# Attention with a relative-position bias, then a max-of-three MoE: bias rows of the later heads written during the attention's first steps

## The chip, the core and the metric

The kernel runs on one core of a Trainium2 chip. The metric is device time in microseconds (us) of one execution, as the median of several runs. TensorE is called PE, VectorE DVE, ScalarE ACT, GpSimd POOL and SyncE SP; SP issues nearly all transfers (DMAs), which 16 DMA engines carry out.

## What is computed

```
scores = q @ k^T / sqrt(64)                          # 4 batches, 8 heads, 576 x 576
x      = log1p(|i - j|) / log1p(max(i, 1))           # depends on the positions alone
bias   = max(x * w1 + b1, 0) @ w2                    # 32 hidden values -> 8 heads
attn   = softmax(scores + bias);  out = attn @ v     # -> 2304 tokens of 512
h      = max(out @ mw1, out @ mw2, out @ mw3)        # 768 columns each
result = h @ mwo                                     # 2304 x 512
```

The bias is the same for the four batches, so it is made once, for all eight heads.

## The kernel before

All is written in the order in which each engine runs it; nothing is scheduled behind the author's back.

**Bias stage.** The 576 query positions are 36 groups of 16. For each group, `hidden` makes four tiles on DVE and ACT (L113, L116), `product` multiplies them on PE into a tile of tag `bp` (L134), and `finish` scales that tile into a tile `bs` of 128 partitions (16 positions x 8 heads, L154 on ACT or L157 on DVE, whichever has less work so far) and writes it to `bias_d` in DRAM (L161, 295.5 KB). The groups run as 32 to 35 and then 0 to 31; group g is finished two turns after its hidden tiles. `bs` has 12 buffers. `bp` has four buffers of two PSUM banks, eight banks in all; one more `bp` tile, `wps`, is taken before the first group for five products that only warm PE up. The bias of the first two heads (`load_bias(0, t)`) is read back from `bias_d`, shifted row by row, into the tiles `bias0` to `bias3` (L169, 128 positions each) and `bias4` (L172, the last 64), while the stage runs. `bias1` is loaded after group 21, `bias2` after group 29, `bias3` at the end.

**Attention.** A unit is two heads of one batch, a pair two units. `Attention.step(n)` starts one tile of 128 rows and ends the one of five steps before: `front` multiplies q and k on PE into two score tiles of tag `s` (L262; L255 in every pair's mixed step, which takes the last 64 rows of both units), `shift` adds the bias tile and takes the row extreme on DVE (L272, `sn` and `nm`), `expo` on ACT (L285), `norm` on DVE and POOL (L294, L297). For the older tile, `flip` turns it on PE (L323), and the products with v (L358) follow in the steps after. `s` has two buffers of two banks, which one step fills. Steps 0 to 4 also run four small PE products that fill time (`warm`, L334). The first pair's steps use the bias tiles 0, 1, 2, 4, 2, 3, 3, 0, 1. `load_qk` (L213, L214) and `load_v` (L239, L240) are issued some steps ahead: `load_qk` in steps 0 and 4 for units 2 and 3, `load_v` in step 7 for unit 1.

**Weights.** From step 8 on, the generator `first` converts the expert weights between the steps: `fetch` (L513) loads them one piece ahead, and ACT's `wa` (L520) is the first use. The first `fetch` is issued when the generator is made, ahead of step 0. The tiles of the pools `xa` and `wpool` lie where the bias stage's tiles lay.

**Transfers.** SP issues in program order. Its transfers take eight semaphores in turn (DMAHW0 to 7), so that each waits until the one eight places before it has landed.

**The border.** The stage's SBUF pool `bias_p` and its PSUM pool are released, and the attention's PSUM pool takes the same eight banks; its first two banks are the first buffer of `s`.

Of the kernel before, what the change touches and what calls it, by code (L numbers as in the profile page):

```python
# [9 lines left out]
F32 = mybir.dt.float32  # L10
# [4 lines left out]
PSUM = bass.MemoryType.PSUM  # L15
# [4 lines left out]
def kernel(  # L20
# [12 lines left out]
    nc = tc.nc  # L33
    B, H, S, D = v.shape
# [3 lines left out]
    NTQ = S // 128  # L38
# [3 lines left out]
    NG = S // 16  # L42
# [4 lines left out]
    psums = []  # L47
# [11 lines left out]
    BW = S + 32  # L59
    bias_d = dram.tile([S * H * BW + 2 * S], F32, name="bias_d")  # L60
# [15 lines left out]
    def bias_setup(pool):  # L76
        sm = pool.tile([128, small.shape[1]], F32, name="sm0", bufs=1)
        one = pool.tile([128, 1], F32, name="one", bufs=1)
        w2s = pool.tile([128, 32], F32, name="w2s", bufs=1)
        bp = pool.tile([128, 4 * NG], F32, name="bp", bufs=1)  # L80
        nw = small.shape[1] - S
        nc.scalar.dma_start(out=sm[:, nw:], in_=small[:, nw:])
        nc.sync.dma_start(out=sm[:, 0:nw], in_=small[:, 0:nw])
        nc.scalar.activation(one, signm.bitcast(F32), ACTF.Exp)
        cuts = (0, 1, 3, 35, 35 + 4 * NG, 35 + 5 * NG, 35 + 5 * NG + S)
        w1c, b1c, w2r, pt, ipo, wl = (sm[:, x:y] for x, y in zip(cuts, cuts[1:]))
        nc.vector.tensor_scalar(out=wl, in0=wl, scalar1=w1c, scalar2=None, op0=ALU.mult)
        nc.vector.tensor_scalar(out=w2s, in0=w2r, scalar1=8.0, scalar2=None, op0=ALU.mult)
        nc.scalar.activation(bp, pt, ACTF.Copy, scale=b1c[:, 0:1])
        make_identity(nc, ident)  # L90

        return dict(wl=wl, w2s=w2s, bp=bp, ipo=ipo)

    def bias_stage(pool):
        k = bias_setup(pool)
        wl, w2s = k["wl"], k["w2s"]
        load = {"dve": 0.0, "act": 0.0}
        hid = {}
        late = {}

        def hidden(g):
            i0 = 16 * g
            nf, nr = S - i0, i0 + 15
            n = max(nf, nr + 1)
            n_act = 1 if load["act"] + (n + 90) < load["dve"] + 4 * (0.52 * n + 130) else 0
            load["act"] += n_act * (n + 90)
            load["dve"] += (4 - n_act) * (0.52 * n + 130)
            hs = []
            for c in range(3, -1, -1):
                m = 4 * g + c  # L110
                h = pool.tile([128, S], F32, tag=f"hid{c}", bufs=4, name=f"hid{m}")
                if c < 4 - n_act:
                    nc.vector.tensor_scalar(out=h[:, 0:n], in0=wl[:, 0:n], scalar1=k["bp"][:, m:m + 1],  # L113
                                            scalar2=0.0, op0=ALU.add, op1=ALU.max)
                else:
                    nc.scalar.activation(h[:, 0:n], wl[:, 0:n], ACTF.Relu, bias=k["bp"][:, m:m + 1])  # L116
                hs.insert(0, h)
            hid[g] = (hs, nf, nr)

        def product(g):  # L120
            hs, nf, nr = hid.pop(g)
            bp = psums[-1].tile([128, 1024], F32, tag="bp", bufs=4, name=f"bp{g}")
            o = 512 - nr if max(nf, nr) <= 512 else 0
            if nr > 512:
                runs = [(0, nr, 512, -1), (512, nr - 512, nr - 512, -1), (nr, 0, nf, 1)]
            elif nf > 512:
                runs = [(0, nr, nr, -1), (nr, 0, 512 - nr, 1), (512, 512 - nr, nr + nf - 512, 1)]
            else:
                runs = [(o, nr, nr, -1), (512, 0, nf, 1)]
            late[g] = bp[:, o:o + nr + nf]  # L130
            for o, d, w, step in runs:
                for c in range(4):
                    src = hs[c][:, d:d + w] if step > 0 else hs[c][:, d:d - w:-1]
                    nc.tensor.matmul(bp[32 * c:32 * c + 32, o:o + w], lhsT=w2s, rhs=src, start=True, stop=True)  # L134


        todo = list(range(NG - LEFT // 16, NG)) + list(range(NG - LEFT // 16))
        for i in range(NG + 2):
            if i < NG:
                hidden(todo[i])  # L140
            if 0 < i <= NG:
                product(todo[i - 1])
            if i > 1:
                x = todo[i - 2]
                finish(pool, k, load, x, late.pop(x))
            yield

    def finish(pool, k, load, g, i):
        bs = pool.tile([128, S + 16], F32, tag="bs", bufs=12, name=f"bs{g}")
        ip = k["ipo"][:, g:g + 1]  # L150
        w = S + 15
        o = bs[:, 0:w]
        if load["act"] + 0.96 * w + 165 <= load["dve"] + 1.04 * w + 185:
            nc.scalar.activation(o, i, ACTF.Copy, scale=ip)  # L154
            load["act"] += 0.96 * w + 165
        else:
            nc.vector.tensor_scalar(out=o, in0=i, scalar1=ip, scalar2=None, op0=ALU.mult)  # L157
            load["dve"] += 1.04 * w + 185
        dst = bass.AP(tensor=bias_d.tensor, offset=bias_d.offset + 16 * g * H * BW,
                      ap=[[H * BW + 1, 16], [BW, H], [1, S + 15]])  # L160
        nc.sync.dma_start(out=dst, in_=bs[:, 0:S + 15])  # L161

    def bias_rows(i, n, h, j, w, nh=1):
        ap = [[H * BW, n]] + ([[BW, nh]] if nh > 1 else []) + [[1, w]]
        return bass.AP(tensor=bias_d.tensor, offset=bias_d.offset + (i * H + h) * BW + 15 + j, ap=ap)

    def load_bias(hp, t):
        if t < NTQ:
            nc.sync.dma_start(out=bias_t[t], in_=bias_rows(128 * t, 128, 2 * hp, 0, S, 2))  # L169
        else:  # L170
            for p in (0, LEFT):
                nc.sync.dma_start(out=bias_t[t][p:p + LEFT], in_=bias_rows(LB, LEFT, 2 * hp, 0, S, 2))  # L172
# [16 lines left out]
    LAG = 5  # L189
# [790 lines left out]
    with tc.manual_schedule():  # L980
# [2 lines left out]
        apool = tc.alloc_tile_pool(name="attn_p", bufs=1, side="right")  # L983
        at = Attention(apool)
        n = 0
        with tc.tile_pool(name="bias_p", bufs=1) as bp:
            warm = bp.tile([128, 256], F32, name="warm")
            nc.vector.memset(warm, 0.0)
            wps = psums[-1].tile([128, 1024], F32, tag="bp", bufs=4, name="wps")
            for _ in range(5):  # L990
                nc.tensor.matmul(wps[:, 0:256], lhsT=warm[:, 0:128], rhs=warm, start=True, stop=True)
            for g, _ in enumerate(bias_stage(bp)):
                if g == 0:
                    at.load_qk(0)
                    at.load_v(0)
                    first = at.prep(0)
                if g in (5, 8):
                    next(first)
                if g == 16:
                    at.load_qk(1)  # L1000
                if g == 33:
                    second = at.prep(1, nc.gpsimd)
                if g in (33, 35):
                    next(second)

                if g == 12:
                    load_bias(0, NTQ)
                if g in (19, 27, 35):
                    load_bias(0, (g - 19) // 8)
            load_bias(0, NTQ - 1)  # L1010
        psums.pop().release()
        psums.append(tc.alloc_tile_pool(name="psum", bufs=1, space=PSUM))
        xa = ctx.enter_context(tc.tile_pool(name="xa", bufs=1, reuse_waits="tile"))
        wpool = ctx.enter_context(tc.tile_pool(name="wpool", bufs=1, reuse_waits="tile"))
        for x in range(NX):
# [171 lines left out]
```

## Time and profile before

| | us |
|---|---|
| median of 3 runs | 580.58 (580.0 to 583.82) |
| profiled execution | 579.1 |
| its span, from the first to the last instruction | 577.3 |
| PE busy / DVE / ACT / POOL | 565.7 / 447.4 / 370.9 / 289.6 |
| granted clock of PE, mean | 1.000 of full speed (2.4 GHz) |

Times in the rows are counted from the span's start. A row of a timeline has the start, the time from the first start to the last end, engine, line and tile, and in brackets how long the engine stood still before and what the profile names as its releaser. That releaser is inferred: where an instruction waits for several semaphores, the one that came last by the profile is named. DMA share is the mean busy share of the 16 DMA engines; the landing of a DMA is counted from the start of its issue.

### The profile page before, as it was taken

How to read it: one execution, taken by the hardware profiler on the slowest of the kernel's cores; microseconds unless marked ns; L12 is line 12 of the kernel's file. 1: busy time of each engine (PE TensorE's matmuls, PEld its weight loads, DVE VectorE, ACT ScalarE, POOL GpSimd, SP SyncE). 2: the span in 40 equal slices, each digit the busy share in tenths (PEclk: the TensorE clock that was granted, in tenths of full speed). 3: DMA queues.
4: the chain of work that ended last, by engine and by line, in shares of the span. 5: the costliest groups of instructions: out<-in, count | busy, mean ns of one | idle time of the engine just before them, and what ended most of it. 6: DMA issues, size and time to landing. Idle time of an engine off the chain costs nothing.

```text
span 577.3 us, 12583 instructions
## 1 busy us (share of the span) xinstructions
PE 565.7 (98%) x4593; PEld 463.1 (80%) x4593; DVE 447.4 (77%) x955; ACT 370.9 (64%) x856; POOL 289.6 (50%) x296
## 2 busy tenths in 40 slices
PE   8998999999999999999999999999999999989997
PEld 4455766667676767676759999999999999979997
DVE  7995679999989999888749876664777235798884
ACT  7996898888889988798747553243233233545552
POOL 1856577687787979786640043362472330720000
PEclk9999999999999999999999999999999999999999
DMA  5898804934593456630010131521223132456662
GB/s 162 229 364 300 259 16 96 353 119 161 151 328 98 156 161 200 192 99 22 23 38 1 55 128 37 177 99 37 73 92 123 51 99 66 144 177 181 185 188 77
DMA packets 72493, 79.61 MB, mean 138 GB/s; under 512 B 22896, under 2 KB 53872, under 8 KB 72432
## 3 DMA queue, kind: packets, MB, share of 16 engines
q1 hardware_dynamic: 72288, 78.52, 43.2%
q8 instruction: 36, 0.59, 0.5%
q10 hardware_dynamic: 144, 0.29, 0.2%
q14 instruction: 25, 0.20, 0.1%
HBM read 50.61 MB, written 27.93 MB: 136 GB/s over the span
## 4 chain that ended last, share of the span: by engine, by line
PE 88%; ACT 5%; DVE 2%; issue 2%; POOL 1%; DMA 1%; DVEq 0%; POOLq 0%
PE pv L358 15%; PE tp L323 12%; PE s L262 11%; PE p L581 10%; PE p L580 10%; PE p L579 10%; PE bp L134 3%; PE p_o L906 3%; PE p_o L904 3%; PE p_o L905 3%; PE s L255 2%; PE c L579 1%; PE c L580 1%; PE c L581 1%; ACT hid L116 1%
## 5 line engine op out<-in xcount | busy, mean ns | idle before, releaser
L297 POOL TENSOR_SCALAR e<-e,rc 128x576 f32<-128x576 f32 x144 | 113.5, 801 | 53.9 <-DVE rc L294 41.0
L285 ACT ACTIVATE e<-sn,nm 128x576 f32<-128x576 f32 x144 | 111.4, 775 | 33.2 <-DVE nm L272 29.6
L272 DVE CUSTOM_DVE_ANT_0 sn<-s,bias 128x576 f32<-128x576 f32 x144 | 103.1, 753 | 21.8 <-PE s L262 16.1
L323 PEld LDWEIGHTS tp<-ident,e 128*128 128x128 f32 x576 | 61.6, 141 | 31.4 <-issue 17.8
L323 PE MATMUL tp<-ident,e 128*128 128x128 f32 x576 | 78.9, 280 | 0.4 <-DVE et L406 0.2
L358 PE MATMUL pv<-et,vt 128*64 128x320 f32 (+1 forms) x496 | 75.2, 419 | 0.1
L471 POOL TENSOR_TENSOR wl<-wr,wh 128x256 fp32r<-128x256 f32 x25 | 22.9, 943 | 95.3 <-ACT wh L663 95.3
L406 DVE COPY et<-tp 128x512 f32<-128x512 f32 (+1 forms) x80 | 49.5, 627 | 17.2 <-PE tp L323 16.5
L358 PEld LDWEIGHTS pv<-et,vt 128*64 128x64 f32 x496 | 31.2, 136 | 24.8 <-issue 11.3
L619 ACT COPY u<-p 128x384 f32<-128x384 f32 x24 | 11.5, 479 | 58.9 <-PE p L581 58.8
L262 PE MATMUL s<-kh,qh 64*128 64x288 f32 x256 | 47.6, 343 | 1.2 <-ACT bs L154 0.9
L229 POOL TENSOR_TENSOR kl<-kr,kh 128x576 fp32r<-128x576 f32 x16 | 40.8, 2550 | 15.6 <-ACT kh L226 15.3
L403 ACT COPY et<-tp 128x512 f32<-128x512 f32 (+1 forms) x72 | 39.5, 548 | 7.7 <-PE tp L323 4.8
L134 PE MATMUL bp<-hid,w2s 128*32 128x79 f32 (+51 forms) x640 | 41.1, 394 | 2.0 <-DVE hid L113 1.1
L113 DVE TENSOR_SCALAR hid<-sm,bp 128x528 f32<-128x528 f32 (+17 forms) x108 | 40.2, 449 | 0.0
L262 PE MATMUL s<-kl,qh 64*128 64x288 f32 x256 | 40.2, 295 | 0.0
L262 PE MATMUL s<-kh,ql 64*128 64x288 f32 x256 | 39.4, 290 | 0.2 <-POOL ql L229 0.2
L134 PEld LDWEIGHTS bp<-hid,w2s 128*32 128x32 f32 x640 | 21.0, 110 | 22.6 <-issue 12.9
L262 PEld LDWEIGHTS s<-kh,qh 64*128 64x128 f32 x256 | 26.2, 184 | 12.9 <-issue 5.0
L471 POOL TENSOR_TENSOR wl<-ws,wh 128x256 fp32r<-128x256 f32 x28 | 27.4, 1008 | 14.6 <-ACT wh L665 11.9
L471 DVE TENSOR_TENSOR q<-p,u 128x384 f32<-128x384 f32 x36 | 19.9, 554 | 17.4 <-ACT u L626 14.9
L626 ACT COPY u<-p 128x384 f32<-128x384 f32 x24 | 11.5, 479 | 32.8 <-PE p L581 32.8
(230 smaller groups left out, 1632.8 us busy)
## 6 DMA issues: line engine op xcount, KB each, us to landing
bias_d<-bs SPq DMA_DIRECT2D x36, 295.5 KB, 5.9
bias<-bias_d SPq DMA_DIRECT2D x16, 576.0 KB, 6.2
w<-in_moe_w_dram SPq DMA_DIRECT2D x36, 256.0 KB, 3.1
h_d<-ht SPq DMA_DIRECT2D x18, 384.0 KB, 3.2
hin<-h_d SPq DMA_DIRECT2D x16, 384.0 KB, 4.4
qr<-in_qd_dram SPq DMA_DIRECT2D x16, 288.0 KB, 5.3
kr<-in_kd_dram SPq DMA_DIRECT2D x16, 288.0 KB, 5.3
vt<-in_v_dram SPq DMA_DIRECT2D x32, 128.0 KB, 3.2
```

What stands on the lines that cost most here:

```text
L134: nc.tensor.matmul(bp[32 * c:32 * c + 32, o:o + w], lhsT=w2s, rhs=src, start=True, stop=True)
L262: nc.tensor.matmul(ss[h][:, x, 0:HALF], lhsT=u[q][p, 128 * t:128 * t + 128], rhs=u[k][p, cols], start=(j == 0), stop=(j == 2))
L272: nc.vector.tensor_tensor_reduce(out=sn.rearrange("p (a b) -> p a b", a=2), in0=st["s"][h][:, :, 0:HALF], in1=bt.rearrange("p (a b) -> p a ...
L285: nc.scalar.activation(st["e"][:, S * h:S * h + S], sn, ACTF.Exp, scale=-1.0, bias=nm, accum_out=st["sm"][:, h:h + 1])
L297: nc.gpsimd.tensor_scalar(out=e, in0=e, scalar1=rc[:, h:h + 1], scalar2=1.0, op0=ALU.mult, op1=ALU.mult)
L323: nc.tensor.transpose(tp[:, 128 * c:128 * c + 128], e2[:, k0:k0 + 128], ident)
L358: nc.tensor.matmul(pv[p], lhsT=w, rhs=x, start=(c == 0), stop=(c == NTQ))
L406: nc.vector.tensor_copy(*x)
L471: eng.tensor_tensor(out=out, in0=f(a), in1=f(b), op=op)
L579: nc.tensor.matmul(o, lhsT=hi[:, c], rhs=h[:, j], start=first and j == 0, stop=False, **on)
L580: nc.tensor.matmul(o, lhsT=hi[:, c], rhs=l[:, j], start=False, stop=False, **on)
L581: nc.tensor.matmul(o, lhsT=lo[:, c], rhs=h[:, j], start=False, stop=last and j == 1, **on)
```

## The change

For the last 14 groups of the stage (18 to 31), `finish` writes only the rows of heads 0 and 1, each with a DMA of its own (16 partitions of the tile, every eighth one). The tile is kept (`bs` has 26 buffers), and its whole group, the first two heads included, is written later: three groups at the end of each of steps 2 to 5 and two in step 6. For that, steps 0 to 6 run ahead of the release of `bias_p`, and the pools `xa` and `wpool` and the first `fetch` come after step 6 rather than before step 0. The attention's PSUM pool is made with `reuse_waits="tile"`: a tile in it waits only for what used its own banks, where before the pool's first tile waited for all.

```diff
-                finish(pool, k, load, x, late.pop(x))
+                finish(pool, k, load, x, late.pop(x), i - 2 >= NG - KEPT)
             yield
 
-    def finish(pool, k, load, g, i):
-        bs = pool.tile([128, S + 16], F32, tag="bs", bufs=12, name=f"bs{g}")
+    KEPT = 14
+    kept = []
+
+    def finish(pool, k, load, g, i, keep):
+        bs = pool.tile([128, S + 16], F32, tag="bs", bufs=12 + KEPT, name=f"bs{g}")
...
-        dst = bass.AP(tensor=bias_d.tensor, offset=bias_d.offset + 16 * g * H * BW,
-                      ap=[[H * BW + 1, 16], [BW, H], [1, S + 15]])
-        nc.sync.dma_start(out=dst, in_=bs[:, 0:S + 15])
+
+        def write(h=None):
+
+            dst = bass.AP(tensor=bias_d.tensor, offset=bias_d.offset + 16 * g * H * BW + (h or 0) * BW,
+                          ap=[[H * BW + 1, 16]] + ([[BW, H]] if h is None else []) + [[1, S + 15]])
+            nc.sync.dma_start(out=dst, in_=bs[:, 0:S + 15] if h is None else bs[h::H, 0:S + 15])
+
+        if keep:
+            for h in range(2):
+                write(h)
+            kept.append(write)
+        else:
+            write()
...
-        with tc.tile_pool(name="bias_p", bufs=1) as bp:
+        bp = tc.alloc_tile_pool(name="bias_p", bufs=1)
...
         psums.pop().release()
-        psums.append(tc.alloc_tile_pool(name="psum", bufs=1, space=PSUM))
+        psums.append(tc.alloc_tile_pool(name="psum", bufs=1, space=PSUM, reuse_waits="tile"))
+        while n < LAG + 2:
+            at.step(n)
+            for f in kept[:3] if n > 1 else ():
+                kept.pop(0)()
+            n += 1
+        bp.release()
         xa = ctx.enter_context(tc.tile_pool(name="xa", bufs=1, reuse_waits="tile"))
```

SP's queue at the end of the bias stage, before (`bs29` is group 29's tile, `bias2` the bias tile 2; in brackets the semaphores waited for):

```order
L161 DMA bias_d_60<-bs28_851 16x8x591 [waits DMAHW6_49,Activation_49]
L161 DMA bias_d_60<-bs29_871 16x8x591 [waits DMAHW7_49,Activation_49]
L169 DMA bias2_76<-bias_d_60 128x2x576 [waits DMAHW1_49,DMAHW0_49]
L161 DMA bias_d_60<-bs30_888 16x8x591 [waits DVE_49]
L161 DMA bias_d_60<-bs31_891 16x8x591 [waits DMAHW2_49,Activation_49]
L169 DMA bias3_77<-bias_d_60 128x2x576 [waits DMAHW5_49,DMAHW4_49,DMAHW6_49,DMAHW3_49,DMAHW7_49,DMAHW2_49,DMAHW1_49]
L513 DMA w643_0_918<-in_moe_w1_dram 128x2x256 x2
L213 DMA qr2_922<-in_qd_dram 128x576
```

The same place of SP's queue in the changed kernel:

```order
L167 DMA bias_d_60<-bs29_882 16x591 [waits DMAHW2_49,Activation_49]
L167 DMA bias_d_60<-bs29_882 16x591 [waits DMAHW3_49]
L182 DMA bias2_76<-bias_d_60 128x2x576 [waits DMAHW4_49]
L167 DMA bias_d_60<-bs30_900 16x591 [waits DMAHW5_49,DVE_49]
L167 DMA bias_d_60<-bs30_900 16x591 [waits DMAHW6_49]
L167 DMA bias_d_60<-bs31_904 16x591 [waits DMAHW7_49,Activation_49]
L167 DMA bias_d_60<-bs31_904 16x591 [waits DMAHW0_49]
L182 DMA bias3_77<-bias_d_60 128x2x576 [waits DMAHW5_49,DMAHW3_49,DMAHW6_49,DMAHW2_49,DMAHW7_49,DMAHW1_49,DMAHW0_49]
L226 DMA qr2_914<-in_qd_dram 128x576
```

Each group's write has become two of 16 rows, and the first weights have left the place behind the load of `bias3`. Further down in the same queue of the changed kernel stand the whole groups:

```order
L227 DMA kr2_913<-in_kd_dram 128x576
L167 DMA bias_d_60<-bs18_646 16x8x591 [waits DMAHW4_49]
L167 DMA bias_d_60<-bs19_667 16x8x591
L167 DMA bias_d_60<-bs20_688 16x8x591
L167 DMA bias_d_60<-bs21_709 16x8x591
L167 DMA bias_d_60<-bs22_731 16x8x591
L167 DMA bias_d_60<-bs23_752 16x8x591 [waits DMAHW1_49]
L226 DMA qr3_1052<-in_qd_dram 128x576 [waits DMAHW2_49,PE_49,Pool_49]
```

They stand between the loads of `qr`/`kr` for unit 2 and for unit 3, and eight more follow behind the latter; DMAHW4 is here the load of `bias2` and DMAHW1 that of `bias3`. On PE, the first score of the attention follows the last products of group 31. Before:

```order
L134 MATMUL bp31_879<-hid127_854,w2s_96 32x80
L262 MATMUL s0_0_0_925<-kh0_242,qh0_318 128x288 [waits DVE_49,Activation_49]
L262 MATMUL s0_0_1_926<-kh0_242,qh0_318 128x288
L262 MATMUL s0_0_0_925<-kl0_243,qh0_318 128x288 [waits Pool_49]
L262 MATMUL s0_0_1_926<-kl0_243,qh0_318 128x288
```

In the changed kernel:

```order
L134 MATMUL bp31_891<-hid127_865,w2s_96 32x80
L275 MATMUL s0_0_0_917<-kh0_242,qh0_318 128x288 [waits Activation_49]
L275 MATMUL s0_0_1_918<-kh0_242,qh0_318 128x288
L275 MATMUL s0_0_0_917<-kl0_243,qh0_318 128x288 [waits Pool_49]
L275 MATMUL s0_0_1_918<-kl0_243,qh0_318 128x288
```

The first score no longer waits for DVE; that wait has moved to the first filler of step 0. The order of the instructions on PE, DVE, ACT and POOL is otherwise as before.

## Rows read from the trace of the kernel before

**Rows 1.** The page: the span, and each engine's busy time (share, instructions).

```profile
span 577.3 us, 12583 instructions
PE 565.7 (98%) x4593; PEld 463.1 (80%) x4593; DVE 447.4 (77%) x955; ACT 370.9 (64%) x856; POOL 289.6 (50%) x296
```

**Rows 2.** Busy us by stretch: length, engines (instructions), PE's clock, DMA share, GB/s.

```profile
27.25:49.76 22.51, 21.36 (x322) 11.69 (x322) 21.12 (x60) 20.63 (x36) 14.84 (x4) 1.00 1.01 356
...
57.11:64.87 7.76, 6.85 (x57) 4.93 (x57) 4.56 (x15) 5.33 (x15) 3.81 (x6) 1.00 0.70 223
...
77.00:100.00 23.00, 23.00 (x207) 15.62 (x207) 20.14 (x56) 20.30 (x55) 15.51 (x18) 1.00 0.25 62
```

**Rows 3.** Chain of waits in order of time: start, us, what.

```profile
48.95 0.76 ACT bs L154
...
49.76 1.11 PE s L262 x11
...
86.53 1.76 PE pv L358 x12
```

**Rows 4.** Timeline of DVE: the first `sn` of steps 1, 2, 4 and 5.

```profile
53.42 0.76 DVE L272 CUSTOM_DVE_ANT_0 sn<-s,bias 128x576 f32<-128x576 f32 x1 [1.03 <-PE s L262]
...
57.11 0.76 DVE L272 CUSTOM_DVE_ANT_0 sn<-s,bias 128x576 f32<-128x576 f32 x1 [2.16 <-PE warm L334]
...
62.37 0.76 DVE L272 CUSTOM_DVE_ANT_0 sn<-s,bias 128x576 f32<-128x576 f32 x1 [0.95 <-PE s L262]
...
64.87 0.76 DVE L272 CUSTOM_DVE_ANT_0 sn<-s,bias 128x576 f32<-128x576 f32 x1 [0.98 <-PE s L262]
```

**Rows 5.** Timeline of PE: step 0's first score, last scores of steps 2 and 5.

```profile
49.76 0.40 PE L262 MATMUL s<-kh,qh 64*128 64x288 f32 x2 [0.87 <-ACT bs L154]
...
55.70 0.29 PE L262 MATMUL s<-kh,ql 64*128 64x288 f32 x1
...
64.64 0.29 PE L262 MATMUL s<-kh,ql 64*128 64x288 f32 x1
```

**Rows 6.** Timeline of SP: issue of the loads of bias tiles 2 and 3.

```profile
49.56 1.50 SPq L169 DMA_DIRECT2D bias<-bias_d  x1
...
58.56 0.36 SPq L169 DMA_DIRECT2D bias<-bias_d  x1
```

**Rows 7.** Landing of these two loads: in the issues at 49.5, by tile at 58.5.

```profile
bias<-bias_d SPq DMA_DIRECT2D x1, 576.0 KB, 7.4
...
DMA to landing us min/median/max: 4.9/4.9/4.9
```

**Rows 8.** Timeline of ACT: copies of groups 18 and 29.

```profile
34.73 0.75 ACT L154 ACTIVATE bs<-bp,sm 128x591 f32<-128x591 f32 x1
...
47.13 0.76 ACT L154 ACTIVATE bs<-bp,sm 128x591 f32<-128x591 f32 x1
```

**Rows 9.** Busy us by other stretches, columns as in rows 2.

```profile
37.00:50.00 13.00, 11.85 (x176) 6.23 (x170) 11.37 (x29) 11.64 (x20) 12.84 (x4) 1.00 1.02 364
...
60.00:72.00 12.00, 11.77 (x101) 9.01 (x101) 8.78 (x28) 9.91 (x28) 6.71 (x10) 1.00 0.93 304
72.00:82.00 10.00, 9.83 (x88) 6.81 (x87) 6.89 (x20) 9.00 (x29) 7.54 (x10) 1.00 0.01 2
```

**Rows 10.** Issue in ns (min/median/max): groups, `vl`, its landing; `vl` in 100 to 330.

```profile
L161 SPq DMA_DIRECT2D bias_d<-bs x18: 522/740/1582, 33.2 to 51.7; - x18
...
L240 SPq DMA_DIRECT2D vl<-in_v_dram x2: 517/522/527, 63.5 to 65.0; - x2
...
DMA to landing us min/median/max: 4.9/5.1/5.4
...
vl<-in_v_dram SPq DMA_DIRECT2D x26, 16.0 KB, 2.6
```

**Rows 11.** Groups by line, 27.25 to 49.76: busy us, mean ns, idle before, releaser.

```profile
L154 ACT ACTIVATE bs<-bp,sm 128x591 f32<-128x591 f32 x18 | 13.6, 756 | 1.8 <-PE bp L134 1.8
```

**Rows 12.** By tile, `wa` from 70 to 110: ns, first and last start.

```profile
L520 ACT ACTIVATE wa<-w x3: 692/705/706, 83.1 to 107.0; 128x512 f32<-128x512 f32 x3
```

More of the change, by code (lines that the diff above doesn't have):

```diff
@@ L985 @@
         n = 0
-        with tc.tile_pool(name="bias_p", bufs=1) as bp:
[L987 to L1010, printed above, removed]
@@ L1011 @@
-        psums.pop().release()
-        psums.append(tc.alloc_tile_pool(name="psum", bufs=1, space=PSUM))
+        bp = tc.alloc_tile_pool(name="bias_p", bufs=1)
+        warm = bp.tile([128, 256], F32, name="warm")
+        nc.vector.memset(warm, 0.0)
+        wps = psums[-1].tile([128, 1024], F32, tag="bp", bufs=4, name="wps")
+        for _ in range(5):
+            nc.tensor.matmul(wps[:, 0:256], lhsT=warm[:, 0:128], rhs=warm, start=True, stop=True)
+        for g, _ in enumerate(bias_stage(bp)):
+            if g == 0:
+                at.load_qk(0)
+                at.load_v(0)
+                first = at.prep(0)
+            if g in (5, 8):
+                next(first)
+            if g == 16:
+                at.load_qk(1)
+            if g == 33:
+                second = at.prep(1, nc.gpsimd)
+            if g in (33, 35):
+                next(second)
+            if g == 12:
+                load_bias(0, NTQ)
+            if g in (19, 27, 35):
+                load_bias(0, (g - 19) // 8)
@@ L1013 @@
+        load_bias(0, NTQ - 1)
+        psums.pop().release()
+        psums.append(tc.alloc_tile_pool(name="psum", bufs=1, space=PSUM, reuse_waits="tile"))
[5 more added lines that the diff above has]
+        bp.release()
         xa = ctx.enter_context(tc.tile_pool(name="xa", bufs=1, reuse_waits="tile"))
```

## Prediction, made before the changed kernel was run

> **What bounds the kernel now.** The page comes first: PE is busy 98% of the span, so time is won only where PE stands still or works on fillers [rows 1]. The busy times by stretch show three stages. The bias stage runs to 49.76 us with the DMA engines full (share 1.01, 356 GB/s). The attention's first steps follow to about 77 us. From 77.00 us PE has no gap at all: 23.00 us busy of 23.00 [rows 2]. The change touches the end of the first stage and the second.
>
> In the chain of waits over that second stage, step 0 begins with PE at 49.76, released by the last bias copy on ACT (48.95 to 49.71), and the chain then goes back and forth between PE's scores and DVE's `sn` [rows 3]. A step's two score tiles use the only two buffers of tag "s", so PE's step n+1 must follow DVE's step n. Undisturbed, this loop takes 2.50 us: `sn` of steps 4 and 5 starts at 62.37 and 64.87. From step 1 to step 2, 53.42 to 57.11, it takes 3.69 us [rows 4].
>
> That long one is step 2, the first to read bias tile 2. The view puts DVE's wait down to PE's fillers (L334), but PE's last score of step 2 had ended at 55.70 + 0.29 = 55.99 [rows 5]. The load of bias tile 2 was issued at 49.56 and took 7.4 us to land, the slowest bias load of the stage: 49.56 + 7.4 = 56.96, and DVE starts 0.15 us later [rows 4, 6, 7]. So I read the wait as this DMA's. It lies behind the last whole groups in a full DMA queue. The load of tile 3, issued when the queue was empty, took 4.9 us [rows 7].
>
> **The change, part by part.**
>
> *Small writes instead of whole groups.* Groups 18 to 31 now write 2 of 8 heads, twice 295.5 / 8 = 36.9 KB instead of 295.5 KB (KB of 1,024 bytes). Copies of groups 18 and 29 start at 34.73 and 47.13 [rows 8], 12.4 us for 11 groups, so one each 1.13 us: the writes' demand falls from 268 to 67 GB/s, where the engines moved 364 in all from 37 to 50 us [rows 9]. The queue drains, and the load of tile 2 meets an almost empty one. For its landing I take 4.9 us, the row nearest to that state; the other end is today's 7.4.
>
> When is that load issued? SP must first issue 24 small writes and the load of tile 1, from 35.5 us (group 18 copied, 34.73 + 0.75) on. No row shows such a write. Bounds: 0.36 us, the issue of tile 3's load into an empty queue, and 0.740 us, the median of the whole-group writes while it was full; a 16 KB load of `vl` took 0.517 to 0.527 [rows 6, 10]. I take about 0.5, nearest to `vl` in size: 24 x 0.5 + 0.4 = 12.4, thus 47.9. The two writes of group 29 cannot be issued before its copy ends at about 47.9 anyway, so the load goes out at about 48.9. It lands at 48.9 + 4.9 = 53.8, before the scores of step 2. DVE then starts with the scores, as in step 5, where `sn` follows the start of the last product by 64.87 - 64.64 = 0.23 us: 55.70 + 0.23 = 55.93 [rows 4, 5]. **Gain: 57.11 - 55.93 = 1.18 us.** It cannot be more, because those scores wait for nothing that the change moves.
>
> *What is late next.* Tile 3 is needed in step 5. Now it is issued at 58.56, after SP waited for the last writes, and lands at 63.46, 1.41 us before DVE uses it at 64.87 [rows 4, 6, 7]. Afterwards its use moves to 63.69, and its load moves to about 54, since it waits only for small writes of groups 24 to 31. No new wait. Steps 3 to 9 form the same chain of PE, DVE, ACT and POOL and move as a whole; then PE is gapless and keeps the gain.
>
> *Larger `bs` pool.* In the stage, ACT's and DVE's copies wait for PE or for nothing, never for a buffer's DMA (18 copies on ACT, 1.8 us idle, all put down to PE) [rows 11]. Gain 0. Its cover is the copy's pace, 1.13 us; without it a copy would wait for a landing.
>
> *Banks one by one.* The `bp` buffers are four of two banks. The fillers' tile takes the first, the groups follow in turn, and the 36th (group 31) falls into the first again: the banks where step 0's scores lie. By the order, PE's first score waited for DVE and ACT and now for ACT, and both times that is group 31's copy ending at 49.71. Gain 0; if that wait did vanish, PE's idle 0.87 us before 49.76 would be the bound [rows 5]. The new wait of the fillers for DVE can only be for group 30's copy, DVE's last work of the stage, on which that first score waited before.
>
> *Whole groups in steps 2 to 6.* SP issues 14 writes of 295.5 KB, 4.24 million bytes (MB), after the loads of tile 3 and of `qr`/`kr` 2, so neither is behind them. The first waits for tile 2's landing (about 54), the sixth for tile 3's (about 59); behind them SP holds `qr`/`kr` 3, the first weights and `vt` 1. The engines are nearly free afterwards (share 0.01 from 72 to 82) [rows 9], and 28 more issues on SP in all delay no compute engine by themselves. The nearest user is ACT's first `wa` at 83.10 [rows 12], then 81.9. Up to those weights 4.24 + 0.59 + 0.52 = 5.35 MB go out; at the 304 GB/s of 60 to 72 us [rows 9] that takes 17.6 us, from 55.5 to 73.1, and with a landing of 4.9 the weights are there at 78. Cost 0, with 4 us to spare. `vt` 1 follows, used by the products at 86.53 [rows 3]. The second write of the two heads adds 14 x 74 KB, 1.06 MB, contained in this.
>
> **Sum.** -1.18 + 0 + 0 + 0 = -1.2 us. The profiled execution took 579.1 us: 577.3 of span and 1.8 around it; it would become 577.9. The median shown is 580.58, 1.5 above the profiled one, so I predict 580.58 - 1.18 = **579.4 us**.
>
> **Rivals.**
>
> *SP falls behind (slower).* Place: the 24 small writes ahead of tile 2's load. Decides when each takes more than 0.67 us: (57.11 - 0.15 - 4.9 - 35.5 - 0.4) / 24. With 0.740 the load is issued at 35.5 + 0.4 + 17.8 = 53.7, lands at 58.6, and step 2 starts at 58.7: +1.6 us, **582.2**. For it: at most eight of SP's transfers are out at once (each names the semaphore of the eighth before it), and `vl` loads of 16 KB took 4.9 to 5.4 us to land in a busy queue [rows 10], an eighth of which is 0.61 to 0.68. Against it: later the same loads land in 2.6 us [rows 10], and the queue is what these writes empty. Chance 0.12. The Trainium skill says in "DMA: Bandwidth & Descriptors", section "Rules for kernel authors", that many small transfers should be joined into a large one and that under 64 KB one pays mostly overhead. By that rule cutting groups into 36.9 KB pieces loses time, and this rival is the form it would take. The trace shows the overhead, 2.6 us for 16 KB [rows 10], but eight at once share it.
>
> *The moved bytes come late (slower).* ACT works in order, so a late weight holds up every exponential behind `wa`. This decides below 5.35 MB / (81.9 - 4.9 - 55.5) = 249 GB/s. At 223, the rate of 57.11 to 64.87 us [rows 2], the weights land at 84.4: 2.5 late, net +1.3, **581.9**. Against it: that stretch's engines were only 0.70 busy; full ones moved 304 to 364 [rows 9]. Chance 0.05.
>
> *No gain.* Step 2 waits for something else, as the view's own label (L334) says, or tile 2 still lands at 7.4 us: 48.9 + 7.4 = 56.3 keeps 0.7 of 1.2. **580 to 580.6**. Chance 0.08.
>
> *More gain.* The banks' waits do let PE start early: a further 0.87, **578.5**. Chance 0.03.
>
> **How the numbers follow.** The forecast (-1.2) keeps 0.72. Its centre is 579.4. The range reaches from 577.8 (the extra 0.87, and 0.7 for the scatter of the runs, which lie between 580.0 and 583.82 before) to 582.4 (both slower rivals). About 1% (5.8 us) is what a measurement of this kernel can tell from no change, and no case reaches it: within 1% 0.96, faster 0.01, slower 0.03 for a stall of SP's queue that I have not seen.
>
> **What the profile after would show.** Right: tile 2's load issued near 49 and landing in about 5 us; DVE's `sn` of step 2 at about 55.9; intervals of 2.5 us in steps 0 to 6 but for the mixed step; PE's first score still at 49.8; DMA share well under 1 from 40 to 49 us and near 1 from 56 to 72; `wa` at about 82 without a DMA wait. Wrong: issues of small writes above 0.67 us each; a load of tile 2 after 52; ACT waiting at `wa`; an `sn` of step 2 still near 57 although its bias had landed, which would mean that I named the wrong releaser.

## The result and the profile after

The changed kernel is slower: 582.70 us median of 20 runs against 580.59 for the kernel before (20 runs), a ratio of 1.0054 with a 95% interval of 1.0037 to 1.0071, so about 3.1 us (2.1 to 4.1); the two medians lie 2.1 apart. The ratio leaves out three runs that were far longer than the others (628.4 us of the changed kernel, 625.61 and 907.91 before). The median lies 0.3 us above the range that was given, and on the other side of the kernel before than forecast; like every case of the prediction it stays within 1%. The profiled execution has a span of 580.2 us where before had 577.3 [rows 1], 2.9 us more, so the trace shows the loss in full.

The page of the changed kernel, as in rows 1:

```profile
span 580.2 us, 12598 instructions
PE 566.4 (98%) x4593; PEld 462.9 (80%) x4593; DVE 448.0 (77%) x955; ACT 371.4 (64%) x856; POOL 290.8 (50%) x296
```

The instructions of each compute engine are the same in number, and their busy times grew by less than 1.3 us. The time lies in a wait, and the place is the one that the prediction spoke of, step 2. The first `sn` of steps 1, 2, 3 and 4 on DVE in the changed kernel (lines stand 13 further down than before):

```profile
53.09 0.76 DVE L285 CUSTOM_DVE_ANT_0 sn<-s,bias 128x576 f32<-128x576 f32 x1 [1.02 <-PE s L275]
...
58.92 0.76 DVE L285 CUSTOM_DVE_ANT_0 sn<-s,bias 128x576 f32<-128x576 f32 x1 [4.31 <-DMA bias<-bias_d]
...
62.71 0.76 DVE L285 CUSTOM_DVE_ANT_0 sn<-s,bias 128x576 f32<-128x576 f32 x1 [2.27 <-PE s L268]
...
65.18 0.76 DVE L285 CUSTOM_DVE_ANT_0 sn<-s,bias 128x576 f32<-128x576 f32 x1 [0.95 <-PE s L275]
```

Step 2 starts at 58.92 instead of 57.11 [rows 4], 1.81 us later, and here the view itself names the load of the bias tile as releaser. From there to step 4 it takes 65.18 - 58.92 = 6.26 us, where before took 62.37 - 57.11 = 5.26 [rows 4]: another 1.00. Together 2.81 of the 2.9 us. Nothing after it gives any back.

Why tile 2 is late is seen on SP. Its timeline in the changed kernel (start, length of the row, what, how many issues in it), which answers rows 6:

```profile
43.05 0.57 SPq L182 DMA_DIRECT2D bias<-bias_d  x1
43.73 10.94 SPq L167 DMA_DIRECT2D bias_d<-bs  x16
54.71 0.58 SPq L182 DMA_DIRECT2D bias<-bias_d  x1
55.39 2.37 SPq L167 DMA_DIRECT2D bias_d<-bs  x4
59.50 0.36 SPq L182 DMA_DIRECT2D bias<-bias_d  x1
```

The load of tile 2 is issued at 54.71 (before 49.56 [rows 6]), behind 16 small writes that took 10.94 us, 0.684 each from start to end. Those 16 by line in the changed kernel (ns of one issue, least, median, most; then from issue to landing):

```profile
L167 SPq DMA_DIRECT2D bias_d<-bs x16: 472/558/1225, 43.7 to 54.1; - x16
...
DMA to landing us min/median/max: 1.8/1.9/3.5
```

A small write lands after 1.9 us and SP needs 0.558 us to issue it, with gaps between. All of the 10.94 us is issuing. The view of SP's waits puts 1.0 of it down to copies and hidden tiles, but its releasers are inferred, and SP stood behind the copies throughout: group 22's copy ended at 39.50 and its first write went out at 43.73, and group 29's, the last ahead of the load, ended at 47.67 and its first write went out at 53.50:

```profile
46.91 0.76 ACT L157 ACTIVATE bs<-bp,sm 128x591 f32<-128x591 f32 x1
```

SP did not wait for landings either: each time the DMA eight places before had landed. The last nine writes, with the DMA engines nearly empty, started 0.63 us apart (49.02 to 54.71). The chain of waits of the changed kernel therefore runs through SP itself:

```profile
54.08 0.59 SPq L167
54.67 0.04 issue
54.71 4.04 DMA bias<-bias_d
...
59.74 2.96 PE s L268 x16
62.70 1.39 PE warm L347 x8
```

Busy times by stretch in the changed kernel, columns as in rows 2; the first two lines answer rows 2, the next two rows 9, and the last is the stretch of the last small writes before the load:

```profile
27.25:49.76 22.51, 21.36 (x322) 11.73 (x316) 20.91 (x59) 20.18 (x35) 15.92 (x4) 1.00 0.74 247
57.11:64.87 7.76, 5.13 (x35) 3.44 (x36) 3.04 (x10) 3.19 (x8) 2.01 (x3) 0.78 0.75 254
37.00:50.00 13.00, 11.85 (x174) 6.34 (x168) 11.14 (x29) 11.42 (x19) 12.84 (x4) 1.00 0.54 183
60.00:72.00 12.00, 11.86 (x91) 8.68 (x90) 7.44 (x25) 8.68 (x25) 6.10 (x9) 0.86 0.97 326
49.50:54.70 5.20, 5.06 (x43) 4.06 (x45) 2.97 (x9) 2.64 (x8) 1.18 (x1) 1.00 0.20 61
```

The DMA engines did empty, as forecast: share 0.54 from 37 to 50 us instead of 1.02 [rows 9], and 0.20 in the stretch in which SP issued the last writes. So the pieces are not slow in the DMA engines, which mostly had nothing to do; SP did not hand them out faster. PE's granted clock in the stretch of steps 2 to 4 fell to 0.78, where before had 1.00 [rows 2]. That is the second part of the loss. PE's timeline of the changed kernel at the mixed step, behind the wait, and where it meets POOL:

```profile
59.74 2.96 PE L268 MATMUL s<-kr,qr 64*64 64x288 f32 x16 [3.01 <-DVE nm L285]
...
78.62 0.40 PE L275 MATMUL s<-kh,ql 64*128 64x288 f32 x2 [0.17 <-POOL ql L242]
```

and the same two places in the kernel before:

```profile
57.93 1.97 PE L255 MATMUL s<-kr,qr 64*64 64x288 f32 x16 [0.85 <-DVE nm L272]
...
75.80 0.40 PE L262 MATMUL s<-kh,ql 64*128 64x288 f32 x2 [0.17 <-POOL ql L229]
```

The same 16 products take 2.96 us instead of 1.97 after PE stood still for 3.01 us. At POOL's `ql` the changed kernel is 78.62 - 75.80 = 2.82 us behind, and keeps that to the end.

### The profile page after: what moved, and what is told of

Its sections match the earlier page's. It is cut to its first block, busy times and chain, and to the rows that moved or that the text cites. A ratio compares the mean times of both kernels' runs of the same rounds, so it can differ in the third digit from the quotient of the medians.

```text
span 580.2 us, 12598 instructions
## 1 busy us (share of the span) xinstructions
PE 566.4 (98%) x4593; PEld 462.9 (80%) x4593; DVE 448.0 (77%) x955; ACT 371.4 (64%) x856; POOL 290.8 (50%) x296
## 4 chain that ended last, share of the span: by engine, by line
PE 87%; DVE 4%; issue 2%; DMA 2%; ACT 2%; POOL 1%; SPq 0%; DVEq 0%; POOLq 0%
PE pv L371 15%; PE tp L336 12%; PE s L275 10%; PE p L594 9%; PE p L593 9%; PE p L592 9%; PE bp L134 4%; PE p_o L917 3%; PE p_o L919 3%; PE p_o L918 3%; DVE hid L113 2%; PE s L268 2%; PE c L592 1%; PE c L594 1%; PE c L593 1%
## 5 line engine op out<-in xcount | busy, mean ns | idle before, releaser
L298 ACT ACTIVATE e<-sn,nm 128x576 f32<-128x576 f32 x144 | 111.4, 775 | 35.5 <-DVE nm L285 29.6
L419 DVE COPY et<-tp 128x512 f32<-128x512 f32 (+1 forms) x80 | 49.5, 627 | 17.9 <-PE tp L336 17.2
## 6 DMA issues: line engine op xcount, KB each, us to landing
bias_d<-bs SPq DMA_DIRECT2D x36, 295.5 KB, 5.2
```

The costliest lines, as they stand in the source:

```text
L298: nc.scalar.activation(st["e"][:, S * h:S * h + S], sn, ACTF.Exp, scale=-1.0, bias=nm, accum_out=st["sm"][:, h:h + 1])
```

## The experiments

**Theory.** SP pays for each DMA that it issues, whatever its size. The 24 small writes ahead of tile 2's load make the load late, and the wait lets PE's clock fall. **Rivals.** Small pieces are slow in the DMA engines; the moved writes or the banks disturb the attention; the wait of step 2 is not the load's. All ratios below are to the kernel before on the same chip in the same hour; its median was 580.59 us beside the changed kernel, 580.04 beside the kernels of early loads, fillers and one write, and 578.48 beside the rest.

| kernel | ratio, 95% interval | median, us | span, us |
|---|---|---|---|
| before | | | 577.3 |
| changed | 1.0054, 1.0037 to 1.0071 | 582.70 | 580.2 |
| changed, one write a group | 0.9983, 0.9965 to 1.0002 | 579.35 | 577.5 |
| the same, banks undone | 0.9987, 0.9975 to 0.9999 | 577.87 | 575.9 |
| before, two halves a group | 1.0175, 1.0151 to 1.0199 | 588.86 | 586.7 |
| changed, last 8 groups alone | 0.9999, 0.9985 to 1.0014 | 578.74 | 576.5 |
| changed, tile 2 loaded early | 1.0051, 1.0022 to 1.0079 | 583.33 | 578.3 |
| before, tile 2 loaded early | 0.9994, 0.9976 to 1.0013 | 579.80 | 578.6 |
| changed, 14 fillers in step 2 | 1.0059, 1.0039 to 1.0079 | 583.26 | 579.6 |
| changed, banks undone | 1.0063, 1.0042 to 1.0083 | 582.71 | 580.6 |

### Half as many issues, the same bytes

The rows of a group are stored in the head order 0, 2, 4, 6, 1, 3, 5, 7 (`w2`'s columns are put in that order), so heads 0 and 1 lie four apart and one DMA writes both; the loads of the bias tiles read them at that distance.

```diff
-            nc.sync.dma_start(out=dst, in_=bs[:, 0:S + 15] if h is None else bs[h::H, 0:S + 15])
+            nc.sync.dma_start(out=dst, in_=bs[:, 0:S + 15] if h is None else bs[0::4, 0:S + 15])
...
-            for h in range(2):
-                write(h)
+            write(0)
```

> The changed kernel with the heads laid out in another order in the bias tiles (0, 2, 4, 6, 1, 3, 5, 7), so that the first pair's two heads are every fourth partition and go out in one DMA of 32 rows per group instead of two of 16. Same bytes, 14 small writes instead of 28. Theory A in its form that the number of issues costs: SP keeps pace with the copies, tile 2's load goes out near 49 and lands near 53, no wait in step 2, 579.4. If SP's time goes with the rows instead of with the number of DMAs: the load still near 54, about 582.7.

SP in this kernel, and the first `sn` of step 2:

```profile
41.76 6.43 SPq L167 DMA_DIRECT2D bias_d<-bs  x8
48.28 0.55 SPq L181 DMA_DIRECT2D bias<-bias_d  x1
...
53.19 0.55 SPq L181 DMA_DIRECT2D bias<-bias_d  x1
```

```profile
55.54 0.76 DVE L284 CUSTOM_DVE_ANT_0 sn<-s,bias 128x576 f32<-128x576 f32 x1 [0.95 <-PE s L274]
```

The load of tile 2 goes out at 48.28, and step 2 starts at 55.54 with PE's scores and waits for no DMA. PE meets POOL's `ql` at 74.24, where before had 75.80: 1.56 us won. This is what the prediction had forecast for the change itself (49, 55.9 and 1.18 us). Bytes, banks and the later whole-group writes are those of the changed kernel. The small writes are 14 instead of 28, each of twice the size (73.9 KB) and with as many rows in all. An issue of such a write took SP 0.542 us (median of ten) where one of half the size took 0.558, so what went away is the number of issues. SP now keeps pace with the copies. The time is at or just below that of before, and about 0.7% below the changed kernel by the two ratios. Why the span does not show the whole 1.56 us stands in the last section.

The same kernel with the attention's PSUM pool as before (`reuse_waits="tile"` left out):

> As the kernel with one small write of both heads for each group (14 instead of 28), but with the attention's PSUM pool waiting as before. Theory (banks do nothing; fewer issues let SP keep pace): tile 2's load at 48 to 49 us, no DMA wait in steps 2 and 5, time 579.3 as with the banks one by one, runs at 577.7 or at 579.4 as the output stage falls into its faster or slower pace. Rival (part of that kernel's small gain came from the banks): 580 us or more, and PE's first score later than 49.6.

Its span is 575.9 us, the shortest of all, 1.4 below before, and its 12 runs lie between 577.67 and 578.89 us. SP issues the load at 48.39 and step 2 starts at 55.74. The ratio to before is 0.9987, and its interval ends at 0.9999: a gain of 0.1% is no more than hinted at. The changed kernel with the banks undone, timed beside it, has 1.0063 (1.0042 to 1.0083), and the two differ only in how the small rows are laid out and written. So joining the writes in pairs gives back about 0.8%.

### Twice as many issues, the same bytes

The kernel before, with each whole group from 18 to 31 written in two DMAs of 8 positions, 147.7 KB each.

```diff
+        if 18 <= g < 32:
+            for x in range(2):
+                nc.sync.dma_start(out=bass.AP(tensor=bias_d.tensor, offset=bias_d.offset + 16 * g * H * BW + 8 * x * (H * BW + 1),
+                                              ap=[[H * BW + 1, 8], [BW, H], [1, S + 15]]),
+                                  in_=bs[64 * x:64 * x + 64, 0:S + 15])
+        else:
+            nc.sync.dma_start(out=dst, in_=bs[:, 0:S + 15])
```

> The kernel before, with the whole group of rows 18 to 31 written by two DMAs of 8 positions each, 147.7 KB a piece: the same bytes, twice as many issues, all pieces far above the small writes' 36.9 KB. Theory (SP pays for each DMA, whatever its size): at 0.68 us an issue tile 2's load goes out near 54.7 us as in the changed kernel, and its landing takes 4 us to today's 7.4; step 2 starts at 58.9 to 62, the time is 582.5 to 585.5. Rival (small pieces are what costs): halves of 147.7 KB cost nothing, tile 2's load goes out at 49.6 and the time is that of before, 580.6.

SP, DVE and the busy times by stretch of this kernel:

```profile
44.85 13.22 SPq L163 DMA_DIRECT2D bias_d<-bs  x16
58.12 0.58 SPq L175 DMA_DIRECT2D bias<-bias_d  x1
```

```profile
64.53 0.76 DVE L278 CUSTOM_DVE_ANT_0 sn<-s,bias 128x576 f32<-128x576 f32 x1 [9.82 <-DMA bias<-bias_d]
...
71.85 0.76 DVE L278 CUSTOM_DVE_ANT_0 sn<-s,bias 128x576 f32<-128x576 f32 x1 [2.01 <-PE s L268]
```

```profile
49.76:57.11 7.35, 6.85 (x60) 5.50 (x58) 2.97 (x9) 3.67 (x10) 2.42 (x3) 1.00 0.52 196
64.87:77.00 12.13, 11.53 (x79) 8.72 (x80) 6.53 (x22) 7.30 (x21) 5.45 (x8) 0.73 0.80 244
```

Both expectations missed. The 16 halves take 13.22 us, 0.83 each, the load goes out at 58.12, and the time is well above my theory's 582.5 to 585.5. The loss is accounted for: step 2 starts 64.53 - 57.11 = 7.42 us later, and from step 2 to step 4 it takes 7.32 us instead of 5.26 [rows 4] under the low clock, 2.06 more: 9.5 in all, and the span grew by 9.4.

But this run is no test of what an issue costs, since the halves changed something else as well. Between 50 and 57.5 us the trace has 8 DMA packets in flight for 71% of the time, 9 or 10 for the rest and never fewer, while the kernel before has 16 or more for 79% of the time from 42 to 49.5 us. The DMA share of 0.52 and the 196 GB/s say the same (before 1.02 and 364 [rows 9]). This reads as a write of 8 positions keeping only 8 of the 16 engines busy, and the 8 never stood still. Why is not shown here. At 196 GB/s a half of 147.7 KB takes 0.77 us, and SP's last ten halves went out 0.77 us apart (50.44 to 58.12). SP's pace is that of the transfers, so what an issue costs cannot be read from it. Neither the theory nor the rival had this in it, and the runs that bear on the theory are the one above and the next.

### Fewer groups in two writes

```diff
-    KEPT = 14
+    KEPT = 8
```

> The changed kernel, but only the last 8 groups (24 to 31) write two heads at once; groups 18 to 23 are written whole again. Theory (SP's issues are the bound): SP comes to the 16 small writes at about 42 us, as in the kernel before, and issues one each 0.68 us, so tile 2's load goes out at 42 + 10.9 = 53 us (changed kernel 54.71, before 49.56), lands 4 to 5 us later, at 57 to 58, and step 2's sn starts there: about 0 to 1 us later than before, a time of 580.6 to 582. The size of the loss goes with the number of small writes ahead of the load. Rival (the number of issues does not matter, what costs is something the first six small groups do to the queue): the load goes out at 50 to 51, as the last copy ends at 49.7, lands by 55.5, and the time is 579.4.

```profile
41.51 10.24 SPq L167 DMA_DIRECT2D bias_d<-bs  x14
51.81 0.57 SPq L182 DMA_DIRECT2D bias<-bias_d  x1
```

```profile
56.12 0.76 DVE L285 CUSTOM_DVE_ANT_0 sn<-s,bias 128x576 f32<-128x576 f32 x1 [1.66 <-DMA bias<-bias_d]
```

Between the two loads stood 12 small and 2 whole writes, not 16 small ones as my expectation counted. They took 0.73 us each, so the load went out at 51.81 rather than 53, landed in 4.15 us, and step 2 started at 56.12, 1.0 before the kernel before. The time is that of before within 0.15%, the span 0.8 shorter. With 0, 12 and 24 small writes ahead of it the load goes out at 49.56, 51.81 and 54.71: how late it goes out follows their number, as the theory has it. With 12, the shorter landing (4.15 for 7.4 us) still outweighs the later issue.

### Is it this load that step 2 waits for

The load of tile 2 was moved ahead of the writes of groups 24 to 31, in the changed kernel and in the kernel before (the edit is the same).

```diff
-            if g in (19, 27, 35):
-                load_bias(0, (g - 19) // 8)
+            if g in (19, 27, 29):
+                load_bias(0, {19: 0, 27: 1, 29: 2}[g])
```

> The changed kernel, but the load of bias tile 2 is issued as soon as group 23 is written, ahead of the small writes of groups 24 to 29. Theory A (SP: every small write takes SP about 0.69 us whatever its size, so that tile 2's load is issued late, at 54.7 instead of 49.6): the load goes out near 46, lands near 50, sn of step 2 starts near 55.6 without a DMA wait, PE's clock stays at 1.00 from 57 to 65, and the time is about 579.4, 1.2 us below the kernel before. Theory B (the whole groups written a second time, 4.2 MB in steps 2 to 6, hold something up): they are all still there, so about 582.7.

> The kernel before, with nothing changed but that the load of bias tile 2 is issued after group 23's write and not after group 29's. If step 2's wait in the kernel before is this load's landing: sn of step 2 starts near 55.9 instead of 57.1, span 576.1, time about 579.4. If that wait is something else (the profile had named PE's fillers): 580.6 as before.

DVE in the kernel before with the early load, steps 2 and 5, and the busy times by stretch around step 6 (the clock before the last two numbers):

```profile
55.82 0.76 DVE L272 CUSTOM_DVE_ANT_0 sn<-s,bias 128x576 f32<-128x576 f32 x1 [0.95 <-PE s L262]
...
65.32 0.76 DVE L272 CUSTOM_DVE_ANT_0 sn<-s,bias 128x576 f32<-128x576 f32 x1 [2.71 <-DMA bias<-bias_d]
```

```profile
64.87:77.00 12.13, 10.58 (x83) 8.04 (x83) 8.32 (x24) 10.11 (x27) 7.24 (x9) 0.86 0.75 242
```

Step 2 starts at 55.82 with PE's scores, 1.29 us earlier. So its wait in the kernel before was this load's, as the prediction read it against the view's label [rows 4]. But SP works in order: it stood until 49.51 for the landing of group 23's write, which the load reads, and the eight writes behind it went out late. Tile 3's load came at 60.89, and the stall moved to step 5. The same happened in the changed kernel (SP stood until 48.52, tile 3's load at 60.23, step 5 at 64.72 after 2.33 us idle). In both, PE's clock fell behind that stall (0.86 on average in the stretch shown). Neither gained, so the times of both expectations missed. The runs of the changed kernel with the early load spread over 7.8 us (578.05 to 585.89), and the profiled one is among the short ones, so its span shows the mechanism and not the size. Its median, 583.33, is near the time that theory B gave, so this kernel alone does not put theory B aside; the kernel with one write a group does, which has the same whole-group writes in steps 2 to 6 and no loss.

### What the clock cost

In step 2 alone PE runs 14 fillers instead of 4 for each of its two tiles, so that it works through most of the wait.

```diff
-            for _ in range(4):
+            for _ in range(14 if n == 2 else 4):
```

> The changed kernel with 14 instead of 4 filler products on PE in step 2, so that PE is busy for about 3.8 us of the wait for bias tile 2. If PE's clock falls because PE stands still in that wait, it stays at 1.00, the mixed step's products take 2.0 us instead of 2.96, and about 1.0 us comes back: span 579.2, time 581.7. If the clock falls for another reason, 582.7 and 2.96 us again.

```profile
55.55 3.39 PE L347 MATMUL warm<-ident 128*128 128x128 f32 x28
60.16 1.97 PE L268 MATMUL s<-kr,qr 64*64 64x288 f32 x16 [1.22 <-DVE nm L285]
```

```profile
57.11:64.87 7.76, 6.46 (x55) 4.84 (x54) 3.31 (x11) 3.66 (x10) 2.59 (x4) 1.00 0.65 212
```

The clock stays at 1.00, the mixed step's products take 1.97 us again, and step 4 follows step 2 after 64.61 - 59.34 = 5.27 us, as before. So the fall was PE's standing still, which it now did for 1.22 us instead of 3.01. The load landed 0.4 us later in this execution, and the span is 0.6 below that of the changed kernel, which together make the 1.0 us. The timed runs do not resolve it (1.0059 against 1.0054, each within 0.2%): that this term is 1 us is shown by the trace alone.

### The banks

The changed kernel with the attention's pool as before:

> The changed kernel with the attention's PSUM pool waiting as before; all else as changed. Theory: the banks cost and bring nothing, the loss lies in SP's many issues; so the time is that of the changed kernel, 582.7 us within the scatter (582 to 583.5), tile 2's load still issued at 54 to 55 us, PE's first score at 49.5 to 49.8. Rival: the waits bank by bank disturb the first steps (PE's first score or the fillers start later); then undoing them brings 0.5 us or more, 582.2 or less, and the first score starts at another time.

Span 580.6 us, ratio 1.0063 where the changed kernel has 1.0054, the intervals overlapping (that the median of 582.71 meets the expected time is chance, since the kernel before took 578.48 beside it); PE's first score at 49.55 and the load of tile 2 at 54.74, as in the changed kernel (49.52, 54.71). The banks one by one bring and cost nothing that can be measured here.

## Why the prediction failed

**The step that failed is "When is that load issued?".** The text put the first small write at 35.5 us, the price of one at 0.5, the end of these issues at 47.9, and the load at 48.9. In the trace SP issues the first small write at 36.9, since it is still behind with the whole groups; the kernel before issued group 18's write at 37.08, which could be read. The first eight take 6.15 us, to 43.05, in a queue that is still full (the first lands after 4.8 us), and the other sixteen 10.94. That is 17.09 / 24 = 0.712 us each, none of it a wait for copies. So: 1.4 us for the start, 24 x 0.212 = 5.1 for the price, and 0.3 for the load of tile 1 give 6.8 on top of 47.9, which is the measured 54.7.

The price 0.5 was a row's own length (`vl`, 0.517 to 0.527 [rows 10]), and by that the row was nearly right: the median here is 0.558. What a queue costs is the distance from one start to the next, with the gaps and the long rows among them (up to 1.225). Even the whole groups of the kernel before went out at 7.45 / 8 = 0.93 us apart while the median of a row was 0.768. With the DMA engines full that distance may be the transfers' as much as SP's, but it could be read beforehand, and it warns that a row's length is too little.

**The rival "SP falls behind" is what happened.** Its threshold was 0.67 us a write, and 0.712 came. That its time, 582.2, was so near 582.7 is in part luck: it issued the load at 53.7 and let it land in 4.9 us, the trace has 54.71 and 4.04, and it had no clock in it. The text gave it 0.12, arguing that the writes themselves empty the queue. They did, and it made no difference: at a share of 0.54, and of 0.20 later, SP still took 0.558 us for an issue. Two of the signs of being wrong that the prediction named came: issues above 0.67 us each, and a load of tile 2 after 52. My eight-at-once argument was for a limit by landings, and the landings (1.9 us) were not the limit. The Trainium skill, "Perfetto Trace Analysis", section What "DMA-bound" means, lists the sequencer of the issuing engine as a bound of its own beside the DMA engines, its time being the making of descriptors and not the moving of data; this trace agrees, with 10.94 us of issues on SP at a DMA share that fell to 0.20. The rule of the Trainium skill's "DMA: Bandwidth & Descriptors", section "Rules for kernel authors", that I weighed had the right sign: writes of 36.9 KB lost time, and joined to 73.9 KB they did not. Its limit of 64 KB is not tested here, since the number of issues changed with the size.

**A term was missing.** No case of the prediction had PE's clock in it; it was put at nothing without a reason. A wait of 4.31 us on DVE leaves PE idle for 3.01, and the products behind it run slower: 1.0 us on top of 1.81. Without this term the time would have lain within the range.

**What held, point by point.** Step 2's wait is tile 2's load: shown by the early load in the kernel before. The landing shortens in an emptier queue: 4.04 us for the 4.9 taken, so this term was right and even too careful. The gain of 1.18 us from a timely load: 1.56 with one write for each group, 1.29 with the early load, so the mechanism of the forecast was real and only SP's pace stood against it. The banks: nothing, as forecast. The copies never waited for a buffer's DMA: ACT's 17 copies waited 2.1 us in all, for PE. Tile 3 did not become late: issued at 59.50, landed in 3.8, and step 5 had no DMA wait. But its issue came at 59.50, not at 54, since SP, late with tile 2, then waited until 59.48 for the last small writes to land behind that load. The whole groups in steps 2 to 6 were harmless: 326 GB/s from 60 to 72 us, above the 249 at which that rival decides, and `wa` starts at 85.93, 2.83 after its place before [rows 12], which is the shift and no wait of its own. PE's first score came at 49.52, 0.24 us earlier than before [rows 5]; with the banks undone it is 49.55, so that is not the banks.

## What to carry to other kernels

Price a queue that issues DMAs by the distance from start to start in a stretch where it is busy, and count its issues as you count bytes: a transfer cut in two can cost its queue twice. When you cut a transfer, look in the trace at how many DMA engines the pieces keep busy. When a transfer is to come earlier, look at what stands ahead of it on its own queue, since that queue works in order and a wait there holds everything behind it. Price a wait of PE with the clock that it loses, and not with its length alone.

## What the chip showed that I had not expected

**An issue costs about the same at any size.** Length of an issue on SP, shortest and median: 0.472 and 0.558 us for 36.9 KB, 0.514 and 0.542 for 73.9 KB (one write a group), 0.570 and 0.656 for 147.7 KB (halves), 0.522 and 0.768 for 295.5 KB (before). In the last two the transfers kept the DMA engines that they used full, so their medians are no price of an issue alone; the shortest ones differ by 0.1 us for eight times the bytes. "DMA: Bandwidth & Descriptors" in the Trainium skill, section "Issuing engines are not separate DMA queues", calls the time to initiate a DMA usually small relative to the DMA itself. Here it is 0.558 us beside 1.9 from issue to landing, and since landings overlap and issues don't, it decides.

**The clock comes back after the work does.** In the halves, after PE had stood still for 8.53 us, the granted clock was 0.50 from 64.5 to 70 us, the lower of its two levels (1.2 GHz of 2.4), and 0.83 from 70 to 74:

```profile
64.50:70.00 5.50, 4.64 (x24) 3.25 (x24) 3.04 (x10) 2.70 (x8) 1.53 (x3) 0.50 0.45 114
70.00:74.00 4.00, 3.88 (x33) 3.16 (x33) 1.52 (x5) 2.30 (x6) 1.94 (x3) 0.83 1.03 377
```

The 16 products then take 2.97 us, as after the 3.01 us of standing in the changed kernel. The length of one pause does not say whether the clock falls: in the kernel before with the early load PE stood still for 1.37 and 0.28 us at step 5, and the granted clock was 0.50 from 67.34 to 70.76 us; with the 14 fillers it stood still for 1.22 us, and the clock stayed at 1.00. What decides between the two is not shown here.

**The output stage has two paces.** In the profiled execution of the kernel with one write a group, the output products (`p_o`) run a little slower than in all others, at a granted clock of 1.00 in both. PE's busy time there and in the kernel before (us, products):

```profile
530.00:555.00 25.00, 25.00 (x215) 1.00 0.56 172
```

```profile
530.00:555.00 25.00, 25.00 (x223) 1.00 0.57 173
```

215 products for 223 in 25 us: the stage gives back the 1.6 to 1.8 us that were won, which is why that span is 577.5 and not about 575.7. Its 12 runs fall into 5 at 577.62 to 578.04 and 7 at 579.33 to 579.81 us, a distance of the same size; the 12 runs of the same kernel with the banks undone (577.67 to 578.89, on another chip) have no such second group. What sets the pace was not found: no clock, wait or transfer in the rows differs. It is also about as large as the change's own forecast, so medians of this kernel that differ by 1 us say little without the trace.
